# Six idle products a tick on TensorE while an attention-plus-MLP kernel loads its weights

## The chip, the cores and the metric

The kernel runs on one core of a Trainium2 chip. The metric is the device time of one execution in microseconds (us). The engines named below are TensorE (PE, with its weight loads PEld), VectorE (DVE), ScalarE (ACT), GpSimd (POOL) and SyncE (SP, which issues transfers). Each engine works through its own instructions in the order in which they were written; between engines, semaphores hold an instruction back until what it reads is there.

## The reference

```python
# q, k, v: (8, 8, 576, 64); top_k = 32; scale = 1/sqrt(64)
scores = scale * q @ k^T
kth    = 32nd largest score of each row
scores = where(scores >= kth, scores, -1e9)
attn   = softmax(scores)
x      = (attn @ v)  ->  (4608 tokens, 512)
h      = x @ w_in                      # 512 -> 2048
out    = (max(h,0) + alpha * min(h,0)) @ w_out
```

So there are 64 heads of 576 x 576 scores, of which each row keeps its 32 largest, and behind them an MLP with a leaky activation whose slope `alpha` differs by hidden unit. The kernel rewrites the MLP: `alpha*h + (1-alpha)*max(h,0)`. The first part is linear in x, so `w_in @ (alpha * w_out)` is multiplied out once, into a 512 x 512 matrix `w_id_b`; the second part uses `w_out_b = (1-alpha) * w_out`.

## The kernel before, in words

**Tiles and ticks.** Heads are taken in pairs, 32 of them, and each pair has nine tiles of 128 score rows, 288 tiles in all. The main loop runs over ticks, with one tile entering at each tick. Nothing is moved by a scheduler: the order on each engine is the order in which the loop writes it (`manual_schedule`). Tiles 0 to 7 of a pair go in units of two, tile 8 alone.

**What one tile goes through.** PE computes its scores `ps` (`scores`, L316, float32) into one of the two score buffers. ACT copies them out with a bias per row, to `b` (`act_b`, L325), which frees the buffer, takes the sign sum `h` (`act_s`, L331) and the exponential `e` (`act_e`, L336). POOL turns the sign sum into `SG` (L341). DVE makes `y` from `b` and `SG` (`flip`, L347), finds the largest values by `max` and `match_replace` (L357, L372, L374), and seven ticks after the scores makes the mask `mk` (L421). POOL multiplies mask and exponential to `w` (L431), a transfer on SP turns it (`wT`, L444), and PE multiplies `wT` with the values (`pu`, `av`, L490); DVE takes the reciprocal of the row sums (`rz`, L507) and ACT writes `xb` (L519).

**What a pair needs first.** `prep_plan` puts its steps at fixed ticks before the pair's first tile: PE transposes q (`pq`, L177) and k (`pk`, L190), each copied out by ACT (L180, L182; L194), then their last 64 rows (`pt`, L198/L199, copied at L202/L203); PE forms `pg` (L208), ACT scales it to `GK` (L212), PE multiplies `pr` from it (`pe_r`, L220), and one tick later DVE multiplies `pr` with q into `P` (`dve_p`, L226 to L228). PE then makes the row statistics `st` (L236 to L242).

**One tick on PE.** First the scores of the next unit, if a unit begins at the next tick; then one step of the `back` queue; then the pair steps and `av` of the tick. What a `back` step has for ACT goes into `after` and is written at the head of ACT's next tick.

**The `back` queue.** It starts with `weight_steps()`: after three opening steps come 32 steps, two for each of the 16 rows of w_out. In the first of the two a row is requested, and every second time a part of w_in, and ACT gets two copies (`w_out2`, L593 and L594: the row times 1-alpha into `w_out_b`, the row times alpha into a corner of `xT`). In the second, PE gets nothing, and now and then a transfer is issued. Twelve steps follow in which PE multiplies `w_id` out, six, six and four products of 128 x 128 by 128 x 512 (`pl`, L601) in each group of three, into the one bank of pool `ps_m`. Only then do MLP steps come. A tick takes one `back` step at this stage, so the 32 row steps fall on ticks 3 to 34 and those of `w_id` begin at tick 35.

Of the kernel before, what the change touches and what calls it, by code (L numbers as in the profile page):

```python
# [9 lines left out]
FP32 = mybir.dt.float32  # L10
# [20 lines left out]
def kernel(  # L31
# [10 lines left out]
    nc = tc.nc  # L42
    B, H, S_, D = q.shape
    NTOK, DM = out.shape
# [34 lines left out]
    w_out_b = const.tile([128, NFT, DM], BF16, name="w_out_b")  # L79
# [14 lines left out]
    ps_m = main.enter_context(tc.tile_pool(name="ps_m", bufs=1, space=PS))  # L94
# [463 lines left out]
    def weight_steps():  # L558
        hold = {}

        def alpha():
            a16 = mlp.tile([NFT, 128], FP32, name="a16", bufs=1)
            nc.sync.dma_start(a16, moe_alpha.rearrange("(t p) -> t p", p=128))
            hold["a16"] = a16

        def alpha1():
            aps = ps_m.tile([128, NFT], FP32, name="aps", tag="misc")
            nc.tensor.transpose(aps, hold["a16"], ident_f[0:NFT, 0:NFT])
            hold["aps"] = aps
            hold["inT"] = mlp.tile([128, NKT, NFT, 128], BF16, name="w_inT", tag="gT", bufs=1)  # L570

        def alpha2():
            nc.scalar.copy(alpha_sb, hold["aps"])
            nc.gpsimd.tensor_scalar(alpha1m, alpha_sb, -1.0, 1.0, ALU.mult, ALU.add)

        def lin(f):
            return xT[:, f // 4, DM * (f % 4):DM * (f % 4 + 1)]

        def w_in(kk):
            for hf in range(0, DFF, 1024):  # L580
                nc.gpsimd.dma_start(w_in_b[:, kk, hf:hf + 1024],
                                    moe_w_in[kk * 128:(kk + 1) * 128, hf:hf + 1024])

        def w_in2(kk):
            nc.sync.dma_start_transpose(hold["inT"][:, kk, :, :], w_in_b[:, kk, :])

        def w_out(f):
            hold[f] = mlp.tile([128, DM], FP32, name="w_stage2", tag="stage", bufs=3)
            nc.sync.dma_start(hold[f], moe_w_out[f * 128:(f + 1) * 128, :])

        def w_out2(f):
            ws = hold.pop(f)
            nc.scalar.activation(w_out_b[:, f, :], ws, AF.Copy, scale=alpha1m[:, f:f + 1])  # L593
            nc.scalar.activation(lin(f), ws, AF.Copy, scale=alpha_sb[:, f:f + 1])  # L594

        def w_id(kk, part):
            if part == 0:
                hold["pl"] = ps_m.tile([128, DM], FP32, name="pl", tag="misc")
            pl = hold["pl"]
            for f in range(6 * part, min(6 * part + 6, NFT)):  # L600
                nc.tensor.matmul(pl, hold["inT"][:, kk, f, :], lin(f),  # L601
                                 start=(f == 0), stop=(f == NFT - 1))

        def w_id2(kk):
            nc.scalar.copy(w_id_b[:, kk, :], hold["pl"])

        yield alpha, None
        yield (lambda: None), None
        yield (lambda: (alpha1(), w_out(0), w_out(1))), alpha2
        for f in range(NFT):  # L610
            yield ((lambda f=f: (w_out(f + 2) if f + 2 < NFT else None,
                                 w_in(f // 2) if f < 8 and f % 2 == 0 else None)),
                   (lambda f=f: w_out2(f)))
            yield (lambda: None), (lambda f=f: w_in2(f // 2) if f < 8 and f % 2 == 1 else None)
        for kk in range(NKT):
            for part in range(3):
                yield ((lambda kk=kk, part=part: w_id(kk, part)),
                       (lambda kk=kk: w_id2(kk)) if part == 2 else None)
# [76 lines left out]
    with tc.manual_schedule(engines={E.PE, E.Activation, E.DVE, E.Pool, E.SP}):  # L695
# [52 lines left out]
        for t in range(-16, 0):  # L748
            for eng in ("act", "pool", "pe", "dve"):
                run(t, eng)  # L750
        scores(0)
        back = deque((a, c, 1.0, 0) for a, c in weight_steps())
        credit = 0.0
        after = deque()
# [229 lines left out]
```

## Time and profile before

| | us |
|---|---|
| median of 3 runs (919.61 to 920.65) | 920.16 |
| the profiled execution | 921.15 |
| its span, first to last instruction | 919.4 |
| DVE busy in the span | 845.6 (92%) |
| ACT busy | 810.4 (88%) |
| PE busy | 752.6 (82%) |
| POOL busy | 430.8 (47%) |

The profile's rows give engine, line of the kernel, operation, `out<-in` by the program's names and a count. In a timeline the first column is the start in us from the beginning of the span, the second the time that the row covers, and what stands in square brackets is the idle time ahead of it and what ended that. A row of the waits gives the total in us, how often, and the longest. A row of windows gives each engine's busy time in a stretch, then the granted clock of TensorE as a share of full speed, the share of DMA time and GB/s.

### The profile page before, as it was taken

The page shows a single profiled execution, that of the slowest core. Times are in us where ns is not written, and L with a number is a line of the kernel's source. Part 1 is how long each engine was busy: PE and PEld are TensorE (multiplying, and loading weights), DVE is VectorE, ACT ScalarE, POOL GpSimd, SP SyncE. Part 2 cuts the span into 40 slices and gives each one's busy share as a digit, 9 for nine tenths or more (in the row PEclk, how much of TensorE's full clock was granted, in tenths as well). Part 3 has the DMA queues.
Part 4 walks back from the last instruction along what each step waited for, and adds up shares of the span by engine and source line. Part 5 has one row for each costly group of instructions (what it writes and reads, how often), then busy time and mean ns, then how long its engine had stood idle before and what let it go on. Part 6 is the DMA issues. An engine that isn't in the chain of part 4 may idle for free. (4 is left out here: it accounts for less than half of the span.)

```text
span 919.4 us, 20883 instructions
## 1 busy us (share of the span) xinstructions
PE 752.6 (82%) x5779; PEld 445.7 (48%) x5779; DVE 845.6 (92%) x5308; ACT 810.4 (88%) x1884; POOL 430.8 (47%) x629
## 2 busy tenths in 40 slices
PE   5765698778958799878968799878978788879996
PEld 3443454444535456445544456444544444534564
DVE  3899989999999999999999999999999877999960
ACT  4999989899989999999999999899998877889832
POOL 0364545555555554555455555555545433455410
PEclk9757879799979999999979999899988989999999
DMA  6699634554556466654556565545547543343451
GB/s 151 122 166 197 146 71 100 110 95 93 127 103 117 91 115 118 121 91 96 130 104 117 85 127 114 110 98 101 129 101 131 104 91 87 76 78 77 98 104 39
DMA packets 343021, 99.52 MB, mean 108 GB/s; under 512 B 335200, under 2 KB 335216, under 8 KB 342896
## 3 DMA queue, kind: packets, MB, share of 16 engines
q1 hardware_dynamic: 340544, 95.71, 53.0%
q0 software_dynamic: 1152, 2.10, 1.7%
q8 instruction: 48, 0.79, 0.4%
q14 instruction: 77, 0.63, 0.2%
q10 hardware_dynamic: 1200, 0.30, 0.2%
HBM read 36.71 MB, written 9.44 MB: 50 GB/s over the span
## 5 line engine op out<-in xcount | busy, mean ns | idle before, releaser
L431 POOL TENSOR_TENSOR w<-mk,e 128x576 bf16<-128x576 bf16 x250 | 319.2, 1277 | 361.2 <-DVE mk L421 198.0
L357 DVE MAX8 C<-y 128x8 f32<-128x96 f32 x1728 | 420.6, 244 | 0.1
L316 PE MATMUL ps<-qkT 64*128 64x288 f32 (+1 forms) x1280 | 248.0, 467 | 27.9 <-ACT b L325 27.3
L325 ACT ACTIVATE b<-ps,NT 128x576 f32<-128x576 f32 x288 | 202.1, 758 | 7.1 <-PE ps L316 6.9
L331 ACT ACTIVATE h<-b 128x576 bf16<-128x576 f32 x288 | 202.7, 704 | 1.7
L642 PE MATMUL ph<-xT,w_in_b 128*128 128x128 bf16 (+1 forms) x960 | 151.4, 301 | 44.2 <-ACT gT L648 36.5
L336 ACT ACTIVATE e<-b 128x1152 bf16<-128x1152 f32 (+1 forms) x159 | 174.2, 1096 | 0.0
L316 PEld LDWEIGHTS ps<-qkT 64*128 64x128 f32 (+1 forms) x1280 | 130.0, 191 | 88.5 <-ACT b L325 51.0
L372 DVE MAX8 L<-C 128x8 f32<-128x48 f32 x864 | 163.4, 189 | 0.1
L347 DVE TENSOR_SCALAR y<-b,SG 128x576 int32<-128x576 int32 x288 | 147.4, 512 | 9.8 <-POOL SG L341 9.4
L421 DVE TENSOR_SCALAR mk<-b,KP 128x576 bf16<-128x576 f32 x282 | 143.8, 510 | 0.0
L660 PE MATMUL pz<-w_out_b,gT 128*128 128x512 bf16 x576 | 138.3, 381 | 0.0
L642 PEld LDWEIGHTS <-w_in_b 128*128 128x128 bf16 x960 | 70.3, 98 | 112.8 <-issue 82.0
L648 ACT ACTIVATE gT<-ph 128x512 bf16<-128x512 f32 x144 | 87.9, 619 | 28.2 <-PE ph L642 26.1
L374 DVE MATCH_REPLACE8 C<-L,C 128x48 f32<-128x48 f32 x576 | 108.9, 189 | 0.0
L490 PE MATMUL pu<-v_bf,wT 128*128 128x65 bf16 (+1 forms) x1600 | 71.3, 201 | 21.8 <-DMA wT<-w 10.5
L660 PEld LDWEIGHTS <-gT 128*128 128x128 bf16 x576 | 53.8, 98 | 70.2 <-issue 13.1
L490 PEld LDWEIGHTS <-wT 128*128 128x128 bf16 (+1 forms) x1600 | 66.6, 105 | 34.9 <-issue 14.8
L341 POOL TENSOR_SCALAR SG<-S_all 128x1 int32<-128x1 f32 x288 | 65.2, 226 | 29.6 <-ACT h L331 29.5
L431 POOL TENSOR_TENSOR wm<-mk,e 128x576 bf16<-128x576 bf16 x32 | 40.8, 1276 | 51.2 <-DVE mk L421 50.0
L331 ACT ACTIVATION_READ_ACCUMULATOR h<-b 128x1 f32 x288 | 62.6, 217 | 0.0
L519 ACT ACTIVATE xb<-pu,rz 128x64 bf16<-128x64 f32 x232 | 55.9, 358 | 7.2 <-DVE L L372 3.0
(102 smaller groups left out, 813.9 us busy)
## 6 DMA issues: line engine op xcount, KB each, us to landing
out_dram<-o_sb SPq DMA_DIRECT2D x35, 256.0 KB, 2.3
st_q<-in_q_dram SPq DMA_DIRECT2D x64, 128.0 KB, 2.9
st_v<-in_v_dram SPq DMA_DIRECT2D x64, 128.0 KB, 2.7
kst<-in_k_dram SPq DMA_DIRECT2D x62, 128.0 KB, 2.8
w_stage<-in_moe_w_out_dram SPq DMA_DIRECT2D x16, 256.0 KB, 3.1
w_in_b<-in_moe_w_in_dram POOLq DMA_DIRECT2D x8, 256.0 KB, 6.7
wT<-w SPq DMA_TRANSPOSE x128, 3.3
st_q<-in_q_dram SPq DMA_DIRECT2D x32, 32.0 KB, 2.7
```

What stands on the lines that cost most here:

```text
L316: nc.tensor.matmul(o_, l_, r_, start=True, stop=True)
L325: nc.scalar.activation(t["b"].rearrange("p (a c) -> p a c", a=2), t["ps"], AF.Identity, bias=NT0[:, p * TPP + j:p * TPP + j + 1], scale=ON ...
L331: nc.scalar.activation(h, tiles[n]["b"], AF.Sign, accum_out=S_all[:, n:n + 1])
L336: nc.scalar.activation(e, tiles[n0]["bu"], AF.Exp, scale=scl)
L347: nc.vector.tensor_scalar(t["y"].bitcast(I32), t["b"].bitcast(I32), FLIP, SG[:, n:n + 1], ALU.bitwise_xor, ALU.bitwise_xor)
L357: return [lambda g=g: nc.vector.max(out=C[:, n % TPP, g, :], in_=t["y"][:, g * SEG:(g + 1) * SEG]) for g in range(NSEG)]
L372: ops.append(lambda r=r, src=src: nc.vector.max(out=L[:, 8 * r:8 * r + 8], in_=src))
L421: nc.vector.tensor_scalar(t["mk"], t["b"], row_limit(n), None, ALU.is_ge)
L431: nc.gpsimd.tensor_tensor(dst, t["mk"], t["e"], ALU.mult)
L490: nc.tensor.matmul(o_, wT[:, 4 * side + c, cs], d["v"][:, 5 * side + c, :], start=(c == 0), stop=(c == 4))
L642: nc.tensor.matmul(hold[f][:, i, :], w_in_b[:, kk, (f + i) * 128:(f + i + 1) * 128], xT[:, kk, c0:c0 + tb], start=(kk == 0), stop=(kk == N ...
L660: nc.tensor.matmul(pz[0:m], hold["gT"][:, f, r0:r0 + m], w_out_b[:, f, :], start=False, stop=(f == NFT - 1))
```

## The change

In the row steps PE now gets products too. `keep_busy(f)` takes the bank of `ps_m`, which is not in use then, and multiplies the first 128 columns of row block f of `w_out_b` with the whole of the same row block, six times, each into the same place. Nothing reads that result. It is called with f-1 in both steps of row f, from f = 1 on, so 15 x 2 x 6 = 180 products are added, six a tick in ticks 5 to 34. They stand in the `back` slot: behind the scores of that tick and ahead of its pair steps and its `av`. They wait for ACT's copy L593 of row f-1, written one tick earlier. All else keeps its order.

```diff
+        def keep_busy(f):
+            fill = ps_m.tile([128, DM], FP32, name="fill", tag="misc")
+            for _ in range(6):
+                nc.tensor.matmul(fill, w_out_b[:, f, 0:128], w_out_b[:, f, :],
+                                 start=True, stop=True)
+
...
         for f in range(NFT):
             yield ((lambda f=f: (w_out(f + 2) if f + 2 < NFT else None,
-                                 w_in(f // 2) if f < 8 and f % 2 == 0 else None)),
+                                 w_in(f // 2) if f < 8 and f % 2 == 0 else None,
+                                 keep_busy(f - 1) if f > 0 else None)),
                    (lambda f=f: w_out2(f)))
-            yield (lambda: None), (lambda f=f: w_in2(f // 2) if f < 8 and f % 2 == 1 else None)
+            yield ((lambda f=f: keep_busy(f - 1) if f > 0 else None),
+                   (lambda f=f: w_in2(f // 2) if f < 8 and f % 2 == 1 else None))
```

## The prediction

> **What bounds the kernel now.** I read the page first, for busy shares and for the clock over the span.
>
> ```profile
> span 919.4 us, 20883 instructions
> ...
> PEclk9757879799979999999979999899988989999999
> ...
> ```
>
> Each digit of PEclk covers 23 us; the low ones stand mostly in slices two to eight, where the weights load. Next I cut out that stage, the stretch behind it, and the stretch in which PE multiplies out `w_id`.
>
> ```profile
> core 0: us, PE busy (x) PEld busy (x) DVE busy (x) ACT busy (x) POOL busy (x), PEclk, DMA share, GB/s
> 29.00:120.00 91.00, 59.49 (x390) 38.01 (x390) 88.22 (x552) 89.72 (x200) 46.55 (x68) 0.70 0.84 158
> 120.00:128.00 8.00, 7.72 (x31) 4.54 (x32) 4.29 (x27) 7.16 (x20) 2.25 (x4) 0.59 0.52 111
> 128.00:160.00 32.00, 29.83 (x255) 17.23 (x253) 31.90 (x202) 29.74 (x69) 16.14 (x22) 1.00 0.42 83
> 200.00:250.00 50.00, 45.54 (x345) 25.07 (x346) 49.84 (x315) 47.66 (x117) 26.07 (x38) 1.00 0.53 108
> ```
>
> ```profile
> L601 PE MATMUL pl<-xT,w_inT 128*128 128x512 bf16 x61 | 15.2, 383 | 0.0
> ```
>
> This last row groups the `pl` products from 126.7 to 160 us. In the loading stage DVE (88.2 of 91) and ACT (89.7) are both full, and PE has 31.5 us free at a mean clock of 0.70. From 200 to 250 us DVE alone is full. So DVE sets the time, and a change is worth what it takes from or adds to DVE's idle time. Where is that idle time? The waits of DVE, and then of ACT, from 20 to 160 us:
>
> ```profile
> DVE y L347 <- POOL SG L341: 5.7, 2, 2.9
> DVE P L228 <- PE pr L220: 3.7, 1, 3.7
> DVE rz L507 <- PE pu L490: 1.8, 1, 1.8
> ...
> ```
>
> ```profile
> ACT w_id_b L605 <- PE pl L601: 2.2, 2, 1.5
> ACT b L325 <- PE ps L316: 1.8, 2, 0.9
> ```
>
> The later of the two waits for SG ends at 26.3 us, before ACT has scaled the first row of w_out and so before any new product can run:
>
> ```profile
> 26.32 0.52 DVE L347 TENSOR_SCALAR y<-b,SG 128x576 int32<-128x576 int32 x1 [2.88 <-POOL SG L341]
> 26.65 0.71 ACT L593 ACTIVATE w_out_b<-w_stage,alpha1m 128x512 bf16<-128x512 f32 x1
> ```
>
> What a faster PE can win is then the wait of 3.7 us, and perhaps the 1.8. Here is the timeline around the first, and just before it the sign that ACT, too, has no lead left:
>
> ```profile
> 117.65 0.25 ACT L331 ACTIVATION_READ_ACCUMULATOR h<-b 128x1 f32 x1
> 118.00 0.21 POOL L341 TENSOR_SCALAR SG<-S_all 128x1 int32<-128x1 f32 x1
> 118.25 0.52 DVE L347 TENSOR_SCALAR y<-b,SG 128x576 int32<-128x576 int32 x1
> ...
> 120.28 2.54 PE L208 MATMUL pg<-kst 128*128 128x130 f32 x10 [0.43 <-ACT qTb L203]
> 121.92 0.81 ACT L325 ACTIVATE b<-ps,NT 128x576 f32<-128x576 f32 x1
> 122.75 2.31 PE L316 MATMUL ps<-qkT 64*128 64x288 f32 x8
> 123.73 0.16 DVE L226 TENSOR_TENSOR km<-GK,bones 128x2 bf16<-128x2 bf16 x1
> 124.99 2.24 PE L601 MATMUL pl<-xT,w_inT 128*128 128x512 bf16 x6
> 127.16 0.43 PE L220 MATMUL pr<-qTb,GK 64*64 64x512 bf16 x4
> 127.52 1.47 PE L601 MATMUL pl<-xT,w_inT 128*128 128x512 bf16 x6
> 127.61 0.82 DVE L228 TENSOR_TENSOR P<-pr,qTb 128x512 bf16<-128x512 f32 x2 [3.71 <-PE pr L220]
> 128.92 1.24 PE L316 MATMUL ps<-qkT 64*128 64x288 f32 x8
> ```
>
> At 120 to 127 us PE runs `pg`, scores and the first six `w_id` products at a low clock, all ahead of `pr`, and DVE stands until 127.6 for it. The same eight score products take 2.31 us there and 1.24 at 128.9; six `pl` take 2.17 from start to next start (124.99 to 127.16) and 1.40 later (127.52 to 128.92). The three rows at 117.65 show the other half: ACT's sum ends at 117.90, SG starts 0.1 later, y directly behind it. ACT is on the edge of holding DVE up.
>
> **The change part by part.** It adds 180 products of the shape of `pl`, removes and moves nothing, and adds no instruction to the other engines and no transfer.
>
> *Load.* The stage's ticks last:
>
> ```profile
> L593 ACT ACTIVATE w_out_b<-w_stage,alpha1m x16: 709/720/770, 26.6 to 117.9; 128x512 bf16<-128x512 f32 x16
> ```
>
> 15 intervals of two ticks in 91.3 us, 3.04 us a tick. PE's own work is 59.49/91 x 3.04 = 1.99 us a tick at clock 0.70. Six products cost 1.40 us at full clock. At the low one I take 1.40 x 2.31/1.24 = 2.6 us, by the ratio that the score products show; the 2.17 us of the first six `pl` lie between, as the clock rose while they ran. Low clock throughout would be 4.6 us into 3.04, so PE would fill up; a full PE ended the low clock at 127 us within 7 us. So I take the clock as full for most of the stage. Then the row 128 to 160 is the model: there PE had 61 of the 64 `pl` (14.2 us at 0.233) and 15.6 us of other work in 32 us, 1.48 us in 3.04. 1.48 + 1.40 = 2.88 of 3.04: PE fits, with 0.16 us a tick to spare, and in that row DVE is busy for 31.9 of 32. The throughput I cost at nothing; its cover is that 0.16.
>
> *Waits added.* The six wait for L593, which stands at the head of ACT's tick before, ahead of the `act_b` that the next scores wait for anyway: nothing. Behind the scores, they push back the pair steps of their tick by 1.4 us. Mostly PE stood idle there for ACT. Three places are different.
>
> *First, behind the transfer wait at 85.8 us.*
>
> ```profile
> 85.78 0.73 PE L490 MATMUL pu<-v_bf,wT 128*128 128x65 bf16 x10 [5.19 <-DMA wT<-w]
> 86.44 2.29 PE L316 MATMUL ps<-qkT 64*128 64x288 f32 x8
> 88.66 0.81 PE L190 MATMUL pk<-ident_f,kst 128*128 128x128 f32 x4
> 88.76 1.37 ACT L325 ACTIVATE b<-ps,NT 128x576 f32<-128x576 f32 x2 [0.95 <-PE ps L316]
> 90.03 0.59 ACT L194 COPY qkT<-pk 128x512 f32<-128x512 f32 x1
> ```
>
> ```profile
> 81.90:85.60 3.70, 0.00 (x0) 0.50 1.12 228
> 85.60:89.00 3.40, 3.22 (x20) 0.50 1.00 206
> 89.00:92.40 3.40, 1.93 (x14) 0.99 0.79 174
> ```
>
> `pu` waits 5.2 us for a transfer. The products of both neighbouring ticks stand ahead of `pu` or behind the scores, so PE stays idle from about 82 and the clock low until 89, as now. The 1.8 us wait of `rz` for this `pu` stays. The scores end as before and ACT's 0.95 stays. Then six products come ahead of `pk`: 88.66 + 1.5 (the first one slow) + 0.7 for `pk` (its 0.81 began slow) = 90.9, and ACT wants `pk` at 90.03. ACT loses 0.9 us. The bounds are 0.7 (all at full clock) and 2.5 (all slow: 2.6 + 1.3); I take 0.9, as the row from 89.00 on shows the clock back at 0.99.
>
> *Second, `pr` near 97 us.*
>
> ```profile
> 95.35 0.79 ACT L325 ACTIVATE b<-ps,NT 128x576 f32<-128x576 f32 x1
> 96.19 1.23 PE L316 MATMUL ps<-qkT 64*128 64x288 f32 x6 [1.67 <-ACT b L325]
> 97.35 0.43 PE L220 MATMUL pr<-qTb,GK 64*64 64x512 bf16 x4
> 97.94 0.68 DVE L228 TENSOR_TENSOR P<-pr,qTb 128x512 bf16<-128x512 f32 x1
> ```
>
> The scores wait for b, which comes 0.9 later, 97.1; then 1.16 of scores, 1.40 of products, 0.43 of `pr`: 100.1 against DVE's 97.94. A new wait of 2.1 us on DVE. ACT doesn't wait, so its lead over DVE grows by that.
>
> *Third, the old 3.7 us.* b at 121.92 comes 0.9 later and ends at 123.6. `pg`, at full clock, is out of the way by then. Six of eight score products behind b, 1.16; `pl`, 1.40; `pr`, 0.43: 126.6 instead of 127.61. DVE, 2.1 us later than before, is there at 123.9 + 2.1 = 126.0 and waits 0.6. The new waits (2.1 + 0.6) stand for the old (3.71): 1.0 us gained, 920.16 - 1.0 = 919.2. The profiled execution, 1.0 above the median, would give 920.2. From 128 us on DVE is full to the end of its work, so the shift stays. ACT's loss at the first place decides: its ends, 0.7 and 2.5, give 919.0 and 920.8.
>
> *A rule beside it.* The Trainium skill, "TensorE: Matmul & The Clock Gate", section "Back-to-back issue gap", gives a sustained roofline of about 131 ns a product of 512 columns in a stream of weight loads and products. By that, six would cost about 0.79 us (an estimate from that page) instead of 1.40, and the sum 918.0 instead of 919.2. The trace differs from the rule: 233 ns a product, by the starts at 127.52 and 128.92.
>
> **The rivals.**
>
> *Faster: ACT is never late.* If the idle time at 82 to 86 us does not bring the low clock, the scores at 86.44 take 1.24 instead of 2.29, ACT's 0.95 goes, and `pk` is there at 86.44 + 1.24 + 1.40 + 0.7 = 89.8, before ACT wants it. Then b of the third place ends at 121.8 and `P` starts at 121.8 + 1.16 + 1.40 + 0.43 = 124.8: 2.8 us gained, 917.4. For it: PE has more to do ahead of that gap than now. Against: the row 81.90:85.60, nothing at all on PE, and a clock of 0.50 through the next 3.4 us.
>
> *Faster: cheap products.* If six products of one and the same weight block overlapped more than `pl` does and took 0.8 us, ACT would lose 0.3 instead of 0.9 at the first place, and where 1.40 now stands in the third 0.6 would go: 919.2 - 1.2 = 918.0. Against: the 1.40 of the row at 127.52. The time by the rule of the Trainium skill's page named above is the same 918.0.
>
> *Slower: PE becomes the bound of the stage.* The margin is 0.16 us a tick, with PE strictly in order between waits for ACT, DVE and transfers. Where PE comes late with scores, ACT waits, and ACT has no lead. It decides from the point where six products and what they hold up cost over 1.56 us a tick. If a quarter of the stage's own work ran at low clock, that would be about 0.25 x (1.99/0.70 - 1.99) = 0.2 us a tick more, 0.05 over: 30 ticks x 0.05 = 1.5 us, and low clock for the products in that quarter too adds 0.25 x 1.2 = 0.3 a tick, 9 us more. I price it at 4 us, 924, between the two, since a full PE brings the clock back. For it: ACT and DVE full in the same stage, as they were not both in the row from 128 to 160 (ACT 29.74 of 32). Against: that row's DVE.
>
> *Slower: the change doesn't do what it says.* With the clock at half throughout, 4.6 us would go into 3.04: 30 x 1.5 = 45 us, 965. Against it: a full PE ended the low clock at 127 us.
>
> **How the numbers follow.** No change to a measurement is about 0.2%, 1.8 us. The forecast (919.0 to 920.8) has 0.42, nearly all within 0.2%; late-free ACT 0.20 and cheap products 0.02, both faster; PE as the bound 0.33 and the low clock 0.03, slower. Faster: 0.20 + 0.02 + 0.03 of the forecast's lower edge = 0.25; same 0.39; slower 0.36. The range runs from 917.0, just below the faster rival, to 924.5, just above the price of the slower one; its tail and the 965 are left out. The likeliest case's own range is 918.0 to 920.8.
>
> **What would show it.** The granted clock from 35 to 120 us: over 0.9, but low around 86 to 89. PE busy there, 85 of 91. ACT waiting at L194 for `pk` near 90 us by 0.9, at `b` by 0.95 as now. DVE's `P` waiting for `pr` by 2.1 near 98 and about 0.6 near 126, with the 3.7 gone. If ACT waits for `ps` or `pk` in many ticks, PE is the bound; if `P` never waits, the faster rival holds. I would be wrong above all if the clock's state at 86 us, or what PE's queue holds up in the fullest ticks, differs from this.

## The result, and the profile after

The changed kernel takes 921.94 us (median), the kernel before 920.03 in runs taken beside it: ratio 1.0024, 95% interval 1.0015 to 1.0033. It is slower by 1.9 us, where the forecast was 919.2 us, 1.0 faster. The profiled execution of the changed kernel took 921.27 us, with a span of 919.4, the same span as before; that coincidence is taken up below.

The page of the changed kernel, span and clock:

```profile
span 919.4 us, 21160 instructions
...
PEclk9798999799988999999988999999987999989999
```

The same stretches as before, in windows (PE, PEld, DVE, ACT, POOL busy, then clock):

```profile
29.00:120.00 91.00, 81.08 (x541) 44.75 (x552) 82.97 (x513) 85.49 (x189) 43.18 (x63) 0.92 0.88 154
120.00:128.00 8.00, 6.58 (x38) 3.53 (x36) 8.00 (x52) 7.97 (x21) 4.36 (x8) 1.00 0.32 62
128.00:160.00 32.00, 30.38 (x246) 16.85 (x250) 31.22 (x200) 30.65 (x71) 15.93 (x22) 1.00 0.54 100
```

The clock did what the change wants: 0.92 against 0.70 in the loading stage. But DVE is busy for 83.0 us there instead of 88.2, and ACT for 85.5 instead of 89.7. The idle time of DVE between 120 and 128 us is gone (8.00 of 8), and more of it has come up earlier. The waits of DVE and of ACT from 20 to 160 us (total, times, longest):

```profile
DVE y L347 <- POOL SG L341: 7.1, 4, 2.9
DVE P L228 <- PE pr L220: 4.5, 3, 1.9
DVE rz L507 <- PE pu L490: 1.5, 1, 1.5
DVE sq L253 <- ACT MM L249: 1.1, 1, 1.1
```

```profile
ACT qkT L194 <- PE pk L190: 4.0, 2, 2.0
ACT w_id_b L611 <- PE pl L607: 1.3, 2, 0.6
ACT b L325 <- PE ps L316: 1.0, 2, 0.5
ACT qkT L180 <- PE pq L177: 0.4, 1, 0.4
```

The first row of ACT is the new one: twice 2.0 us for `pk`. On DVE, `P` waits three times instead of once, and y twice more for SG, which needs ACT's sums. Where this begins, on PE and then on ACT:

```profile
54.60 0.48 PE L490 MATMUL pu<-v_bf,wT 128*128 128x65 bf16 x10
58.55 0.49 PE L490 MATMUL pu<-v_bf,wT 128*128 128x65 bf16 x10 [3.46 <-DMA wT<-w]
58.97 1.33 PE L316 MATMUL ps<-qkT 64*128 64x288 f32 x8
60.23 2.74 PE L599 MATMUL fill<-w_out_b 128*128 128x512 bf16 x6
62.77 0.92 PE L190 MATMUL pk<-ident_f,kst 128*128 128x128 f32 x4
```

```profile
63.72 0.59 ACT L194 COPY qkT<-pk 128x512 f32<-128x512 f32 x1 [2.03 <-PE pk L190]
...
94.48 0.59 ACT L194 COPY qkT<-pk 128x512 f32<-128x512 f32 x1 [1.98 <-PE pk L190]
```

PE stands from 55.1 to 58.6 us for a transfer. The clock stays up through that, falls as the six products begin, and they take 2.74 us instead of 1.47. The windows of PE (busy, clock) show the delay of one stretch between idleness and clock:

```profile
53.20:56.60 3.40, 1.89 (x20) 1.00 1.19 162
56.60:60.00 3.40, 1.45 (x18) 1.00 1.13 164
60.00:63.40 3.40, 3.40 (x11) 0.50 1.13 207
63.40:66.80 3.40, 3.35 (x21) 1.00 1.01 200
...
83.90:87.30 3.40, 0.61 (x13) 1.00 1.12 224
87.30:90.70 3.40, 2.55 (x18) 0.50 0.94 146
90.70:94.10 3.40, 3.18 (x10) 0.50 1.28 221
94.10:97.50 3.40, 3.40 (x22) 1.00 0.94 207
```

From 84 us on the same happens again, and there the low clock lasts two stretches. By the end of the stage the loss is there to be read on DVE: `y` of tile 40 (counted from 0) starts 2.6 us later than in the first profile before. The row of the kernel before, and that of the changed one:

```profile
142.25 0.51 DVE L347 TENSOR_SCALAR y<-b,SG 128x576 int32<-128x576 int32 x1
```

```profile
144.87 0.50 DVE L347 TENSOR_SCALAR y<-b,SG 128x576 int32<-128x576 int32 x1
```

### The profile page after: what moved, and what is told of

Its sections match the earlier page's. It is cut to its first block, busy times and chain, and to the rows that moved or that the text cites. A ratio compares the mean times of both kernels' runs of the same rounds, so it can differ in the third digit from the quotient of the medians.

```text
span 919.4 us, 21160 instructions
## 1 busy us (share of the span) xinstructions
PE 771.0 (84%) x5876; PEld 453.7 (49%) x5959; DVE 845.5 (92%) x5308; ACT 810.0 (88%) x1884; POOL 430.3 (47%) x629
## 5 line engine op out<-in xcount | busy, mean ns | idle before, releaser
L316 PE MATMUL ps<-qkT 64*128 64x288 f32 (+1 forms) x1280 | 240.3, 460 | 14.0 <-ACT b L325 13.5
L650 PE MATMUL ph<-xT,w_in_b 128*128 128x128 bf16 (+1 forms) x928 | 148.6, 298 | 46.0 <-ACT gT L656 37.1
L316 PEld LDWEIGHTS ps<-qkT 64*128 64x128 f32 (+1 forms) x1280 | 126.2, 188 | 70.9 <-ACT b L325 33.6
L668 PE MATMUL pz<-w_out_b,gT 128*128 128x512 bf16 x560 | 135.4, 382 | 1.6 <-issue 1.3
```

Of the source, the lines that this page charges most:

```text
L316: nc.tensor.matmul(o_, l_, r_, start=True, stop=True)
L650: nc.tensor.matmul(hold[f][:, i, :], w_in_b[:, kk, (f + i) * 128:(f + i + 1) * 128], xT[:, kk, c0:c0 + tb], start=(kk == 0), stop=(kk == N ...
L668: nc.tensor.matmul(pz[0:m], hold["gT"][:, f, r0:r0 + m], w_out_b[:, f, :], start=False, stop=(f == NFT - 1))
```

## The experiments

The theory (T): six products at low clock, behind a transfer wait and ahead of what ACT needs next, make ACT wait, and ACT has no lead to give. The rivals: PE is too full over the whole stage, so the load itself costs the time (R1); or the time is decided in the stretch from 700 us on (R2). Some kernels stand there with several profiles, since one execution turned out not to stand for all.

**Without the products of two ticks (skip_two).** The changed kernel with nothing added in ticks 14 and 23.

```diff
-  keep_busy(f - 1) if f > 0 else None
+  keep_busy(f - 1) if f > 0 and f != 10 else None      # first step of a row: tick 23
...
-  keep_busy(f - 1) if f > 0 else None
+  keep_busy(f - 1) if f > 0 and f != 5 else None       # second step: tick 14
```

> Six products a tick as in the changed kernel, but none in ticks 14 and 23, the two ticks behind the long transfer waits of pu. T (place and clock: the loss is made where six products at low clock stand ahead of pk): ACT's two waits of 2.0 us at L194 go, DVE's y of tile 40 starts 1 to 2 us earlier than in the kernel before (142.25 us there, 144.87 with the change), time 918.5. R1 (PE is too full over the whole stage): only 12 of 180 products are gone, time stays near 921.9. R2 (the loss lies in the stretch from 700 us on and the stage doesn't matter): y of tile 40 moves as T says, time stays near 921.9.

Measured: 921.68 us, 1.0031 (1.0019 to 1.0042). ACT's waits for `pk` went, as T says, and y of tile 40 came at 142.76, 2.1 us earlier than in the first profile with the change. But it is not earlier than before, and the time stayed where R1 and R2 had put it, not at T's 918.5. In this profile `pu` got its transfer at 88.1 us (85.8 in the profile before), and the scores behind it ran at low clock; the wait of ACT for them:

```profile
91.08 1.37 ACT L325 ACTIVATE b<-ps,NT 128x576 f32<-128x576 f32 x2 [2.29 <-PE ps L316]
```

So the wait for `pk` is one form of the loss, not the only one.

**The two ticks alone (only_two).** Products in ticks 14 and 23, none elsewhere (`f == 10` and `f == 5`).

> The six products in ticks 14 and 23 alone. T: ACT waits about 2 us for pk in at least one of the two, the old wait of P for pr near 127 us stays, y of tile 40 comes 2 to 4 us later than 142.25, time 922 to 924. R1: 12 products in two ticks are nothing, time 920.0. R2: time 920.0 whatever y of tile 40 does.

Measured: 920.69 us, 1.0003 (0.9992 to 1.0014). ACT waited 1.3 us for `pk`, at one place, and y of tile 40 came at 143.9, 1.6 later than in the first profile before. That is T's direction, but less than the 2 to 4 us that it gave; and this profile took 922.68 us, the slowest of the eleven executions. Over all of them the time doesn't differ from before: it is R1's and R2's 920.0, not T's 922 to 924.

**Behind the pair steps (behind, behind_again, behind_again_2).** All 180 products, issued after the pair steps and `av` of their tick.

```diff
...
-  keep_busy(f - 1) if f > 0 else None
+  late.append(f - 1) if f > 0 else None                # both steps
...
             run(n, "pe")
+            while late:
+                busy[0](late.pop(0))
```

> All 180 products, but behind the pair steps and av of their tick instead of ahead of them. T: ACT no longer waits for pk, P no longer waits for pr near 73 and 103 us, near 128 us it waits less than the old 3.7; y of tile 40 at 140 to 141.5, time 918 to 919. R1: the same load on PE, so time near 921.9 and ACT waiting for ps instead. R2: near 921.9 or 920 whatever y of tile 40 does.

> All products behind the pair steps, once more. If these lose in a way of their own, ACT waits for ps by 3 us or more (six slow products behind pu stand ahead of the next scores) and y of tile 40 is over 143.5. If not, y of tile 40 stays within 1 us of 142.1 and the time's excess lies behind 160 us.

> The same, a third profile: ACT's wait for ps and y of tile 40 rise and fall together if the products' place makes the loss.

Measured: 923.48 us, 1.0039 (1.0024 to 1.0054), slower than the change as it was; the repeats took 923.50 and 924.51. No wait for `pk` is left, but now the products behind `pu` stand ahead of the next scores. ACT in the third profile:

```profile
ACT b L325 <- PE ps L316: 6.0, 4, 2.9
```

In the three profiles ACT waits for `ps` by 2.8, 4.3 and 6.0 us, and y of tile 40 comes at 142.08, 144.21 and 145.54. To stand behind the pair steps doesn't help, as the scores of the next tick are as urgent. T's forecast of 918 to 919 was wrong, and R1's (no gain in time, and ACT waiting for `ps` instead) came true. The forecast for the third profile, that waits and y rise together, held.

**More products, so that PE isn't idle (full_wait, full_wait_again).** 20 instead of 6 in ticks 13 and 22, ahead of the `pu` that waits.

```diff
...
-  keep_busy(f - 1) if f > 0 else None
+  keep_busy(f - 1, 20 if f == 5 else 6) if f > 0 else None    # first step of a row: tick 13
...
-  keep_busy(f - 1) if f > 0 else None
+  keep_busy(f - 1, 20 if f == 9 else 6) if f > 0 else None    # second step: tick 22
```

> The changed kernel with 20 products instead of 6 in ticks 13 and 22, ahead of the pu that waits for a transfer, so that PE works through most of that wait; 28 products more. T (the low clock behind the wait makes the loss): the clock stays full to 94 us, six products in ticks 14 and 23 take 1.4 to 1.5 us instead of 2.74 and about 2.5, ACT's two waits for pk of 2.0 us fall to under 0.5, y of tile 40 comes at 141 to 142.5 instead of 144.87, time 919 to 920. R1 (PE too full): 28 more products make it slower, ACT waits as long or longer, time 922 to 925.

> 20 products in ticks 13 and 22, once more. T: if the long row of products itself runs at low clock, it ends late, pq comes late for ACT at L180, and y of tile 40 is over 143; if at full clock, 141 as in the first profile.

Measured: 921.63 us, 1.0009 (0.9992 to 1.0026). The times lie in two groups, 918.2 to 920.0 and 921.6 to 924.4. T had 919 to 920, R1 922 to 925; the median fits neither. The two profiles (919.91 and 920.38 us) are of or near the first group. PE in the first profile, with its busy time and clock from 40 to 120 us:

```profile
79.55 6.00 PE L599 MATMUL fill<-w_out_b 128*128 128x512 bf16 x26
86.92 0.49 PE L490 MATMUL pu<-v_bf,wT 128*128 128x65 bf16 x10 [0.61 <-DMA wT<-w]
87.34 1.24 PE L316 MATMUL ps<-qkT 64*128 64x288 f32 x8
88.51 1.47 PE L599 MATMUL fill<-w_out_b 128*128 128x512 bf16 x6
89.82 0.60 PE L190 MATMUL pk<-ident_f,kst 128*128 128x128 f32 x4
```

```profile
40.00:120.00 80.00, 76.75 (x541) 1.00 0.88 158
```

With 28 products more, the clock doesn't fall between 40 and 120 us, the scores take 1.24 us at this place and the six 1.31 from start to next start. ACT's waits for `pk` fall from 4.0 to 0.9 us, of which 0.25 at the two places, and y of tile 40 comes at 141.01 and 141.36. In the profiles that is the sharpest evidence against R1: PE is busier, and the loss is gone. In time it is weaker: the ratio is 1.0009 where the changed kernel, timed beside it (again), has 1.0042, but its interval overlaps that of the 22 executions above (1.0015 to 1.0033). What makes the upper group, seven of the twelve times, wasn't seen, as neither profile fell in it.

**Only behind both waits (late_only).** Products in ticks 24 to 34 (`f > 10` and `f > 9`).

> Products in ticks 24 to 34 alone, behind both transfer waits. T: no wait of ACT for pk, P waits about 1.2 us near 98 us and under 1 near 126, y of tile 40 1.5 to 2 us earlier than the kernel before (142.25), time 918.2. R1: products cost by their number, 66 of 180 of the loss, time 920.7.

Measured: 919.39 us, 0.9984 (0.9971 to 0.9997), a little faster than before (T had 918.2, R1 920.7). No wait of ACT for `pk` or `ps`, and y of tile 40 at 139.37, 2.9 us earlier than in the first profile before and 1.6 earlier than in the two others.

**The old wait by itself (wid_behind).** The kernel before, without products; in tick 35 the pair steps come ahead of `w_id`.

```diff
+            if n == 35:
+                run(n, "pe")
             first = True
             while back and credit > 0.0 and (first or n >= N0 - 30):
```

> The kernel before, without products; only in tick 35 the pair steps stand ahead of the six products of w_id. Measures what the wait of 3.7 us was worth. By the rows of before, pr can start at 125.0 when the slow scores end, so P at 125.4 instead of 127.6: y of tile 40 2.2 us earlier, at 140.0. T (a shift of DVE at 130 us lasts to the end): time 917.8. R2 (the stretch from 700 us on takes it up): time 920.0.

Measured: 918.27 us, 0.9987 (0.9977 to 0.9997), where T had 917.8 and R2 920.0; y of tile 40 at 140.45. Moving six products out of the way of `pr` gets what 180 products were to get. A shift made at 125 us reaches the end on average, against R2. `P` in this profile waits for half as long as the 3.7 us of the first profile before:

```profile
125.16 0.82 DVE L228 TENSOR_TENSOR P<-pr,qTb 128x512 bf16<-128x512 f32 x2 [1.78 <-PE pr L220]
```

**Both together (late_wid).** Products in ticks 24, 25 and 27 to 34, and the pair steps first in tick 35.

> Products in ticks 24, 25 and 27 to 34 only, and in tick 35 the pair steps ahead of the products of w_id: the two findings put together. T: no wait of ACT for pk, none of P near 98 and 126 us over 0.3, y of tile 40 at 138.5 to 139.5 against 142.25 before, time 916.5 to 918. R1 (products cost by their number): 60 of 180 of the loss against the gain of the pair steps, about 919.

Measured: 917.92 us, 0.9985 (0.9972 to 0.9997), y of tile 40 at 139.01. The longest wait of `P` was 0.5 us, a little over what T gave; the rest came as T had it. With wid_behind and late_only it forms a group a little faster than the kernel before; the three can't be told apart, so no gain of the two moves together shows.

**The same two kernels again (again, again_2, again_3, before_again, before_again_2).**

> The changed kernel once more, for a second profile. The clock changes at multiples of 3.4 us that lie differently to the work in each execution. If the place of these steps decides the size of the loss, y of tile 40 lies between 143 and 147 and not at 144.87 to a tenth, and the span follows it.

> The changed kernel a third time, for its profile: y of tile 40 between 143 and 146, ACT waiting for pk by 1.5 to 4 us in all.

> The changed kernel a fourth time: ACT's wait for pk at L194 and y of tile 40 on one line with the three before (4.0 us and 144.87, 1.9 and 143.25, 1.8 and 140.78).

> The kernel before once more, for a second profile. Where the steps of the clock lie differently, the stretch from 700 us on takes up to 2.3 us less than in the first profile, and y of tile 40 stays within 1 us of 142.25.

> The kernel before a third time, for its profile: y of tile 40 between 140.5 and 142.5, no wait of ACT for pk.

The changed kernel's time beside again was 923.83 us, 1.0042 (1.0030 to 1.0054). Of what was expected of these profiles, again_2 (y of tile 40 between 143 and 146) and before_again (within 1 us of 142.25) missed, and in again the span didn't follow y. The profiles come from more than one chip. The table has, for each profile, the sum of ACT's waits for PE from 30 to 165 us (for `pk`, `ps` and `pq`; those for `pl` lie behind the stage and are left out), the start of y of tile 40, and the time of that execution.

| profile | ACT waits for PE, us | y of tile 40 at, us | time, us |
|---|---|---|---|
| before, first | 1.8 | 142.25 | 921.15 |
| before_again | 1.4 | 140.98 | 920.60 |
| before_again_2 | 1.6 | 140.99 | 920.47 |
| changed, first | 5.4 | 144.87 | 921.27 |
| again | 3.9 | 143.25 | 923.75 |
| again_2 | 1.8 | 140.78 | 920.40 |
| again_3 | 4.2 | 143.64 | 920.02 |
| skip_two | 3.8 | 142.76 | 920.91 |
| only_two | 3.5 | 143.89 | 922.68 |
| behind | 2.8 | 142.08 | 921.44 |
| behind_again | 4.7 | 144.21 | 923.50 |
| behind_again_2 | 6.0 | 145.54 | 924.51 |
| full_wait | 1.3 | 141.01 | 919.91 |
| full_wait_again | 0.9 | 141.36 | 920.38 |
| late_only | 0.0 | 139.37 | 919.36 |
| wid_behind | 1.6 | 140.45 | 916.80 |
| late_wid | 1.2 | 139.01 | 917.84 |

In the kernels with products, each microsecond that ACT waits for PE goes with a y of tile 40 that is later by about one: 139.4 at none, 145.5 at 6.0. (In those before, and in only_two, the old wait at 127 us comes on top. late_wid lies 1.6 below the line: there the pair steps come first in tick 35, and ACT's waits, at 31 and 43 us, lie ahead of its first products.) The means over the profiles, 143.1 for the changed kernel's four and 141.4 for the three before, differ by 1.7, beside 1.9 in the medians of the runs. This is the evidence for what T has left after the experiments: not the place ahead of `pk` as such, but ACT's waits on a PE that comes late out of a transfer wait, at low clock, with six more products in its row. The waits also lie where this says: in the four profiles of the changed kernel, every wait of ACT for PE between 32 and 130 us falls at 59.8 to 64.7 or at 90.0 to 94.5 us, behind the two transfer waits, and nowhere else. That, full_wait and late_only speak against R1. For R1 speaks that its times came nearer than T's in skip_two, only_two and behind. So it isn't excluded that a smaller part of the loss is PE's load; the runs don't separate that from the clock.

R2 is right in one thing. The last column doesn't follow y of tile 40 in each execution: the first profile of the changed kernel makes up its 2.6 us later, again doesn't. The stretch from 700 to 860 us, first before, then changed, then again (PE, PEld, DVE, ACT, POOL busy, clock):

```profile
700.00:860.00 160.00, 133.38 (x1001) 74.13 (x1000) 142.25 (x881) 134.87 (x310) 73.13 (x104) 0.96 0.46 92
```

```profile
700.00:860.00 160.00, 133.79 (x1004) 75.24 (x1017) 144.13 (x894) 136.13 (x313) 74.14 (x106) 0.96 0.46 94
```

```profile
700.00:860.00 160.00, 133.05 (x1001) 73.78 (x999) 141.13 (x873) 133.64 (x308) 72.58 (x104) 0.96 0.45 93
```

DVE is idle for 16 to 19 us there, in waits for PE, POOL and ACT, and how much differs by 3 us between two executions of the same kernel. The medians average over that, one profile doesn't: the equal spans of the two first profiles were such a case.

## Why the prediction was wrong

- **The clock** (over 0.9 from 35 to 120 us, low around 86 to 89): right, 0.94, and low from 87.3 to 94.1. Not foreseen was the low stretch from 60.0 to 63.4.
- **PE's load** (85 of 91 us busy, waits for `ps` not many): 81.1, and 1.0 us. The rival of PE as the bound of the stage did not come about as it was described: ACT waited at two places, not in many ticks.
- **The waits added by L593, costed at nothing**: no row shows one.
- **The third place** (the 3.7 us become 0.6): right, 0.68. But the 3.7 was that of one execution: in the two other profiles of the kernel before, `P` waits 2.5 us there, at 126.3, and 0.6 to 0.7 near 98. And summed from 20 to 160 us, `P` waits 3.4 to 4.5 us in the four profiles of the changed kernel, against 3.1 to 3.7 before: the old wait went, others came.
- **The second place** (a new wait of P of 2.1 near 98 us): 1.90, at 103.7. And there was one more of 1.90 at 72.9, for the same reason, which the prediction didn't have. The three rows:

```profile
72.89 0.82 DVE L228 TENSOR_TENSOR P<-pr,qTb 128x512 bf16<-128x512 f32 x2 [1.90 <-PE pr L220]
...
103.65 0.82 DVE L228 TENSOR_TENSOR P<-pr,qTb 128x512 bf16<-128x512 f32 x2 [1.90 <-PE pr L220]
...
130.23 0.82 DVE L228 TENSOR_TENSOR P<-pr,qTb 128x512 bf16<-128x512 f32 x2 [0.68 <-PE pr L220]
```

- **The first place** (ACT loses 0.9 us, bounds 0.7 and 2.5, once). This is the step that failed. The mechanism was right; the term of the sum was too small, and it was counted once instead of twice. For its size, "the row from 89.00 on shows the clock back at 0.99" took the old timing for the new: in the changed kernel's profile the transfer came later (88.1 us), the clock came back only at 94.1, and the wait was 2.0, between its bounds but near the upper one. And the same place exists a second time, at 58.6 us, behind the other transfer wait. The prediction passed over it with "Mostly PE stood idle there for ACT"; in the profile before PE waited 1.59 us for that transfer, in the changed kernel's 3.46, and the clock fell there too. Twice 2.0 and 1.4 at other waits, 5.4 in all, against the 0.9 + 0.95 that the sum had: 3.6 us more, which turned 1.0 us of gain at tile 40 into 2.6 of loss. ACT's b of the third place shows the same: it was to come 0.9 us later than its 121.92 and came 4.4 later. The second transfer wait, and that b:

```profile
88.15 0.73 PE L490 MATMUL pu<-v_bf,wT 128*128 128x65 bf16 x10 [3.64 <-DMA wT<-w]
```

```profile
126.36 0.80 ACT L325 ACTIVATE b<-ps,NT 128x576 f32<-128x576 f32 x1
```

- **"From 128 us on DVE is full to the end of its work"**: wrong. It is full to about 700 us. On average the shift lasts, as wid_behind shows, but one execution can hide it.
- **The transfer's arrival** was taken as fixed. In the profiles of kernels without products the second half of `pu` starts between 55.4 and 57.3 us at the first wait and between 85.0 and 85.8 at the second; with products, between 56.0 and 58.6 and between 84.5 and 88.6 (full_wait left out, where PE itself is later). The second start goes with what ACT had lost at the first place: where ACT waited for PE by up to 1.2 us between 59 and 65 us, it lies at 84.5 to 85.8; where by 1.6 to 3.5, at 86.7 to 88.6. So part of the second loss seems to follow from the first. No run tries that, nor why the first start moves.
- **The rule beside it** (131 ns a product): the 26 products above take 6.00 us, 231 ns each. The trace does not bear it out, and the rival of cheap products did not come about.
- **The faster rival** (ACT never late, 2.8 us gained by 125 us): it did not come in the changed kernel, but late_only, where ACT never waits for PE, has y of tile 40 2.9 us earlier than the first profile before. In time that was less: 0.16%, about 1.5 us.

## What to carry to other kernels

Filler work that holds a clock up is free only as long as those who wait for PE have lead. Here ACT had none, and six products ahead of what it needed made it wait where the clock had dropped all the same. Look first for the one wait that the low clock causes: moving six real products behind the step that is waited for won 0.13% (0.03 to 0.23), without any filler. And a place that recurs with each period of the loop must be priced at every recurrence, the ones that cost nothing in the trace of before among them.

## What the runs showed of the hardware

In these traces the granted clock changes in steps of some 3.4 us, one step after PE's idleness, and the steps lie differently to the work from one execution to the next: with the change, the second fall is at 87.3 us in the first profile. In again_2 the clock falls at about 84.8 us, while PE waits, and is nearly back when the six products of the second place begin (windows of PE, busy and clock, and the row of the products):

```profile
81.40:84.80 3.40, 0.95 (x15) 1.00 1.10 233
84.80:88.20 3.40, 2.79 (x18) 0.57 1.19 201
88.20:91.60 3.40, 3.40 (x19) 0.93 1.04 221
```

```profile
88.30 1.64 PE L599 MATMUL fill<-w_out_b 128*128 128x512 bf16 x6
```

They take 1.64 us there, and ACT waits 0.6 us for `pk` instead of 2.0.

The Trainium skill, "TensorE: Matmul & The Clock Gate", section "What's actually happening", says that the activity window is 3413 ns long and free-running, so that it doesn't restart with the kernel. The traces agree: in the first profile of the changed kernel the clock falls at 60.0 and 87.3 us and comes back at 63.4 and 94.1, so one, seven and two such windows lie between these points; and ACT's waits for PE in four profiles of one kernel add up to anything between 1.8 and 5.4 us. Idle doesn't have to mean wholly idle: in that first profile the clock fell behind a stretch with 1.45 us of 3.4 busy (56.6 to 60.0 above) and stayed up behind one with 1.89.
